# One gate for all tokens in expert 0's first steps, the routing maximum in PSUM, and a third head step before the last routing's products

## The chip, the cores and the metric

The kernel runs on one NeuronCore of one Trainium2 chip. The metric is device time in microseconds (us) of one launch, the median of the runs; lower is better. The engines are named as the profile names them: PE (TensorE's matmuls; PEld its weight loads), DVE (VectorE), ACT (ScalarE), POOL (GpSimd) and SP (SyncE, which issues most transfers). The granted clock in the profile's rows is a share of TensorE's full rate: 1.00 is 2.4 GHz, 0.50 is 1.2 GHz.

## The reference

Three layers follow one another.

1. A linear attention with a decay for each channel: 4 sequences of 768 tokens, 8 heads of width 48. Per token, `y = r · (state + (u*k) v^T)` and `state = w * state + k v^T`. The result is a matrix `x` of 3072 tokens by 384.
2. A mixture of 8 experts with one expert for each token. `logits = x @ w_gate` and `e_idx = argmax(logits)`. The token's output is `relu(x @ w1[e]) @ w2[e]`, multiplied by the softmax probability of the chosen expert and by `sigmoid(x @ w_output_gate)[e]`. The product of these two factors is what is called the gate value below.
3. A dense gated layer on all tokens: `(silu(x @ w_gate) * (x @ w_val)) @ w_out`, inner width 1536, from weights given as 64-bit floats.

All in 32-bit floats.

## The kernel before

**Attention.** The 3072 tokens are 24 tiles of 128 (`NTILE`), six for each sequence (`NCH`). One loop of 27 iterations runs all stages of the tiles in a skewed order, and inside it the order of the instructions of PE, DVE, ACT and POOL is the order of the program (`manual_schedule`). In iteration `i`, POOL makes products for tile `i+2` (`scaled_k`, L456 to L461), DVE reduces them to `cb` for tile `i+1` and ACT spreads them (`bonus`, L482 and L486), PE makes the scores and outputs (`scores`, `outputs`), and tile `i-2` is written out (`rows_out`, which runs `emit`). `emit` (L122) transposes the tile's result with 32 small matmuls into the PSUM tile `psx`; ACT copies the tokens (`xt`, L127, which SP then stores to `x_d`) and the partial logits (`lh`, L130), and DVE sums these to `lg` (L132): 8 routing logits and 8 logits of the output gate for each token.

**Routing.** When the six tiles of a sequence are done, the generator `route` is put on a list. Each call of `advance` runs one step of the first generator on that list, so the routing's small DVE instructions lie between those of the attention. A step marked TENSOR issues matmuls and runs only where `advance(TENSOR)` is called. `route` takes the row maximum (L144, `mx`), compares (L147, `key`), makes the one-hot `oh`, the counts `cum` (L167), a first group of products for the ranks (`psp`, L171 to L184), some arithmetic, and a second group of products (`psw`, L219) that gives the token lists `rows_f`. Most of its small tiles lie in one PSUM bank (`in_bank`). POOL's operands are all in SBUF.

**Gates.** `gate` (L230) makes the gate values of a group of tiles from `lg` and `mx`: 14 DVE instructions and two exponentials on ACT. For the sequences 0 and 1 it is put on the same list behind their routing. For the sequences 2 and 3 (12 tiles) the logits and the maximum lie at the end of a large SBUF tile (`lg_far`, `mx_far`, L567 and L568), and one gate over both runs in expert 0's first steps, three pieces in each step (`next(gates, None)` in `MoE.run`).

**Expert 0's head.** The first 256 tokens of expert 0 come from the first three sequences, so they are gathered and multiplied while the last sequence is still routed. `moe.head` is a generator of 8 steps, one for each 128 of the inner width 1024. Step `f` issues 9 matmuls into `pha` (L1208; two PSUM buffers in turn), a relu on ACT (L1227), a low part on DVE (L1228), and, from the third step on, the 9 matmuls of step `f-2` into `pya`. Behind the loop the order is by hand: seven pieces of the last routing, two head steps, the products for the ranks, five pieces, a head step, three pieces, a head step, the second products, two pieces (L671 to L680). Then the other tokens of expert 0 are gathered, `in_order` sorts the experts in steps that alternate with head steps, and the gathered tokens are transposed.

**Weights.** Operands of the experts are split in a high part (a cast on ACT, L1084) and a low part (a subtraction, L1085, here on POOL). For expert 0 this is done in the last iterations; `SPLITS` says which parts in which iteration.

**Experts and dense layer.** From there a scheduler orders the instructions by a simulated timeline: 8 experts with 416 to 360 tokens, beside them the conversion of the 64-bit weights, then the dense layer in blocks of 512 tokens.

Of the kernel before, what the change touches and what calls it, by code (L numbers as in the profile page):

```python
# [38 lines left out]
def moe_kernel(ctx, tc, cst, small, tok, tr, u, w1, w2, m_gate, m_val, m_out, out):  # L39
# [79 lines left out]
    def emit(yT, x_rows, lg, pool, ps_x):  # L119


        psx = ps_x.tile([P, 2, 8, 64], F32, name="psx", tag="x")  # L122
        for q, (j, k) in itertools.product(range(NP), ((0, 0), (1, 1), (0, 1), (1, 0))):
            pr, ts = slice(64 * j, 64 * j + 64), slice(64 * k, 64 * k + 64)
            nc.tensor.matmul(psx[ts, j, q, :], lhsT=yT[pr, q, ts], rhs=unit[pr, q, :], start=True, stop=True)
        xt = pool.tile([P, NP, 2, D], F32, name="xt")
        nc.scalar.copy(xt.rearrange("p q j d -> p j q d"), psx[:, :, 0:NP, 0:D])  # L127
        nc.sync.dma_start(out=x_rows, in_=xt.rearrange("p q j d -> p (q j d)"))
        lh = pool.tile([P, 2, NP, G], F32, name="lh")
        nc.scalar.copy(lh, psx[:, :, 0:NP, D:])  # L130
        yield
        nc.vector.reduce_sum(lg, lh.rearrange("p j q e -> p e (j q)"), axis=AX.X)  # L132
# [97 lines left out]
    def gate(sl, lg, mx, pool, sm):  # L230
# [3 lines left out]
        bc = lambda t: t.rearrange("p (c o) -> p c o", o=1).to_broadcast([P, n, E])  # L234
        ex = pool.tile([P, n, E], F32, name="ex")
# [67 lines left out]
    def scratch(pool, **kw):  # L303
        return lambda name, *dims: pool.tile([P, *dims], F32, name=name, **kw)


    with ExitStack() as actx:
# [95 lines left out]
        def tables():  # L403

            nc.gpsimd.memset(ones_b, 1.0)
            nc.gpsimd.memset(yd_all[:, used[0] :], 0.0)
# [158 lines left out]
        routing, gates, now = [], [], [0]  # L565
        far = slice(NTILE - 2 * NCH, NTILE)
        lg_far = yd_all[:, KD * YW - 2 * NCH * G :].rearrange("p (c g) -> p c g", g=G)  # L567
        mx_far = yd_all[:, KD * YW - 2 * NCH * (G + 1) : KD * YW - 2 * NCH * G]  # L568
        assert used[0] <= KD * YW - 2 * NCH * (G + 1)
# [22 lines left out]
        def rows_out(i):  # L592
            g = next(g for g in groups if g.start <= i < g.stop)
            n, late = g.stop - g.start, g.stop > NTILE - NCH
            if i == g.start:
                at = i - far.start
                if at < 0:
                    lgs[i] = apool.tile([P, n, G], F32, name="lg"), in_bank("mx", n)
                else:
                    lgs[i] = lg_far[:, at : at + n, :], mx_far[:, at : at + n]  # L600
            lg, mx = lgs[g.start]
            yield from emit(S.pop(i), x_d[i * P : (i + 1) * P, :], lg[:, i - g.start, :], apool, ps_x)
            if i + 1 == g.stop:
                routing.append((route(g, lg, mx, apool, in_bank, in_bank), 0, 0))
                if late:
                    gates.append((far, lg_far, mx_far))
                elif g.stop == NTILE - NCH:
                    routing.append((head_tokens(), 0, 0))
                else:
                    routing.append((gate(g, lg, mx, apool, in_bank), 0, 0))  # L610
# [10 lines left out]
        with tc.manual_schedule(engines=set(engines)):  # L621
# [50 lines left out]
            next(head)  # L672
            next(head)
# [11 lines left out]
            for _ in range(KF - 4):  # L685
                next(order, None)
                next(head)
            both = ps_x.tile([P, 2, 512], F32, name="pt01", tag="x")
# [91 lines left out]
    moe.run(sorted_positions, lambda pool: (x for g in gates for x in gate(*g, pool, scratch(pool))), ffn)  # L780
# [660 lines left out]
SPLITS = {21: ((0, 0),), 22: ((0, 1),), 23: ((1, 0), (1, 1)), 24: ((2, 0), (2, 1)), 25: ((3, 0),), 26: ((3, 1),)}  # L1441
# [113 lines left out]
```

## Time and profile before

| What | us |
|---|---|
| Median of 3 runs (801.03, 801.21, 805.11) | 801.21 |
| The profiled execution, its own time | 802.04 |
| The profiled execution, span from first to last instruction | 800.3 |
| PE busy in the span | 780.0 |
| DVE busy | 500.8 |
| ACT busy | 346.9 |
| POOL busy | 218.6 |

The busy times are shares of the whole span and mix stages with different limits: the attention up to about 122 us, the head of expert 0 to about 145, the experts to about 345, the dense layer to the end. The section with rows below is by stretch. In a timeline a line is: start, duration, engine, line of the kernel, operation, tiles with their shape, how many instructions were joined, and in brackets how long the engine had stood idle before it and what ended that.

### The profile page before, as it was taken

The numbers are of one execution on the slowest core, as the hardware profiler recorded it, in microseconds if no ns is written. First come the engines' busy times: TensorE is split into PE (matmuls) and PEld (weight loads), VectorE is DVE, ScalarE is ACT, GpSimd is POOL, SyncE is SP. The second block draws the span as 40 slices with busy tenths as digits, with TensorE's granted clock in tenths as the row PEclk, the third lists the DMA queues.
The fourth block names the chain that finished last, engine by engine and source line by source line (L and its number), as shares of the span: only waits on it lengthen the run. The fifth ranks groups of instructions, "written<-read, shape, count | busy, mean of one in ns | idle before, by whom it ended". The sixth has DMA issues, their size and how long they took to land.

```text
span 800.3 us, 15595 instructions
## 1 busy us (share of the span) xinstructions
PE 780.0 (97%) x5982; PEld 717.0 (90%) x5983; DVE 500.8 (63%) x1067; ACT 346.9 (43%) x789; POOL 218.6 (27%) x213
## 2 busy tenths in 40 slices
PE   8989988999999999999999999999999999999997
PEld 4888878999999999988888888888888888899997
DVE  7889976789999899788553335334433543344543
ACT  5878772656566666655332122212221222122322
POOL 6999975535232422120002000200100020001000
PEclk8999998999999999999999999999999999999999
DMA  8999972966778785564301000000000000000000
GB/s 322 309 340 304 332 245 95 316 201 203 262 230 256 234 248 175 152 180 141 107 15 40 1 0 14 40 1 0 36 18 1 8 40 1 1 8 40 1 20 25
DMA packets 61860, 99.28 MB, mean 124 GB/s; under 512 B 5461, under 2 KB 48105, under 8 KB 61776
## 3 DMA queue, kind: packets, MB, share of 16 engines
q1 hardware_dynamic: 58320, 88.34, 33.8%
q0 software_dynamic: 3456, 9.85, 3.7%
q8 instruction: 49, 0.80, 0.4%
q14 instruction: 35, 0.29, 0.1%
HBM read 81.64 MB, written 16.53 MB: 123 GB/s over the span
## 4 chain that ended last, share of the span: by engine, by line
issue 54%; PE 16%; DVE 6%; POOL 4%; DMA 3%; ACT 1%; POOLq 0%; SPq 0%; DVEq 0%; ACTq 0%
PE ph L1208 6%; PE py L1208 5%; POOL out_dram L1380 2%; DMA rw<-m 1%; DMA m<-ab 1%; PE pya L1208 1%; PE pha L1208 1%; DVE ab L1059 1%; PE pt L1177 1%; DVE w1l L1085 1%; POOL xg L1163 1%; DVE w2l L1085 1%; POOL x L1056 1%; DVE ab L1055 1%; PE ph L1204 1%
## 5 line engine op out<-in xcount | busy, mean ns | idle before, releaser
L1404 PE MATMUL pg<-x,wh 128*128 128x512 f32 (+1 forms) x504 | 146.5, 358 | 0.0
L1409 DVE TENSOR_TENSOR hv<-pg,hv 128x512 f32<-128x512 f32 (+1 forms) x84 | 51.5, 614 | 142.0 <-ACT hv L1408 141.9
L1404 PE MATMUL pv<-x,wh 128*128 128x512 f32 (+1 forms) x504 | 137.7, 358 | 0.0
L1380 POOL DMA_INDIRECT out_dram<-ot,tokd x24 | 24.9, 1036 | 407.3 <-DVE ot L1379 403.7
L1408 ACT ACTIVATE hv<-pg 128x512 f32<-128x512 f32 (+1 forms) x84 | 45.0, 536 | 158.8 <-PE pg L1404 158.5
L974 ACT CAST hh<-hv 128x512 fp32r<-128x512 f32 (+1 forms) x84 | 47.0, 560 | 136.7 <-DVE hv L1410 136.7
L1404 PEld LDWEIGHTS pv<-x,wh 128*128 128x128 f32 x504 | 89.9, 188 | 13.9
L1404 PEld LDWEIGHTS pg<-x,wh 128*128 128x128 f32 x504 | 90.2, 188 | 11.3
L1371 PE MATMUL po<-wh,hl 128*128 128x384 f32 x288 | 97.1, 338 | 0.0
L1371 PE MATMUL po<-wh,hh 128*128 128x384 f32 x288 | 96.8, 336 | 0.0
L1371 PE MATMUL po<-wl,hh 128*128 128x384 f32 x288 | 96.8, 336 | 0.0
L1404 PE MATMUL pg<-x,wl 128*128 128x512 f32 (+1 forms) x252 | 90.3, 358 | 0.0
L1404 PE MATMUL pv<-x,wl 128*128 128x512 f32 (+1 forms) x252 | 90.3, 358 | 0.0
L1208 PE MATMUL ph<-x,w1h 128*128 128x416 f32 (+6 forms) x336 | 87.5, 341 | 0.0
L1208 PE MATMUL py<-h,w2h 128*128 128x416 f32 (+6 forms) x336 | 82.3, 341 | 0.0
L975 DVE TENSOR_TENSOR hl<-hv,hh 128x512 fp32r<-128x512 f32 (+1 forms) x84 | 51.7, 615 | 43.6 <-ACT hh L974 43.3
L1410 DVE TENSOR_TENSOR hv<-pv,hv 128x512 f32<-128x512 f32 (+1 forms) x84 | 51.6, 615 | 38.9 <-PE pv L1404 38.3
L486 ACT ACTIVATE dsb<-cs,cb 128x128 f32<-128x128 f32 x192 | 58.8, 389 | 19.5 <-DVE cb L482 19.4
L1208 PEld LDWEIGHTS ph<-x,w1h 128*128 128x128 f32 x336 | 61.5, 188 | 0.2
L1208 PEld LDWEIGHTS py<-h,w2h 128*128 128x128 f32 x336 | 60.7, 188 | 0.5 <-DVE h L1228 0.3
L1056 POOL TENSOR_TENSOR low<-low,exw 128x384 f32<-128x384 f32 x30 | 33.0, 1101 | 98.8 <-DVE exw L1052 78.7
L1208 PE MATMUL ph<-x,w1l 128*128 128x416 f32 (+6 forms) x168 | 58.4, 347 | 0.5 <-DVE h L1228 0.5
(254 smaller groups left out, 1509.8 us busy)
## 6 DMA issues: line engine op xcount, KB each, us to landing
r<-in_w_dram SPq DMA_DIRECT2D x64, 384.0 KB, 4.2
yd_all<-in_tr_dram SPq DMA_DIRECT2D x24, 512.0 KB, 5.2
yd_all<-in_tok_dram SPq DMA_DIRECT2D x24, 384.0 KB, 5.7
rw<-m SPq DMA_DIRECT2D x36, 192.0 KB, 2.7
yd_all<-in_tok_dram SPq DMA_DIRECT2D x24, 256.0 KB, 5.8
m<-ab SPq DMA_DIRECT2D x30, 192.0 KB, 4.4
x_d<-xt SPq DMA_DIRECT2D x24, 192.0 KB, 4.3
cva<-in_w_gate_dram SPq DMA_DIRECT2D x10, 384.0 KB, 4.5
```

The costliest lines, as they stand in the source:

```text
L486: nc.scalar.mul(dsb[:, h, :], ident, cb[:, h : h + 1])
L974: first = nc.scalar.copy(hi, src)
L975: second = nc.vector.tensor_tensor(out=lo, in0=src, in1=hi.bitcast(F32), op=ALU.subtract)
L1056: nc.gpsimd.tensor_tensor(out=low, in0=low, in1=ex.bitcast(F32), op=ALU.mult)
L1085: (engine or nc.vector).tensor_tensor(out=lo, in0=r, in1=hi.bitcast(F32), op=ALU.subtract)
L1208: nc.tensor.matmul(dst[:, 0:n], lhsT=a, rhs=b, start=start and t == 0, stop=stop and t == 2)
L1371: mm = nc.tensor.matmul(po[t], lhsT=a[:, t * P : (t + 1) * P], rhs=bb, start=(f == 0 and j == 0), stop=(f == KF2 - 1 and j == 2))
L1380: st = nc.gpsimd.indirect_dma_start(out=out[:, :], out_offset=bass.IndirectOffsetOnAxis(ap=tokd[:, i : i + 1].bitcast(U32), axis=0), in_=o ...
L1404: nc.tensor.matmul(dst, lhsT=a[:, fs], rhs=bb[:, q, :], start=(q == 0 and j == 0), stop=(q == KD - 1 and j == 2))
L1408: nc.scalar.activation(hv, pg, AF.Sigmoid)
L1409: nc.vector.tensor_tensor(out=hv, in0=pg, in1=hv, op=ALU.mult)
L1410: nc.vector.tensor_tensor(out=hv, in0=pv, in1=hv, op=ALU.mult)
```

## The change

- `emit`: ACT copies `lh` before `xt`; the store of `xt` is issued behind both.
- `rows_out`: for all four sequences the logits lie at the end of the large SBUF tile (`lg_all`, 24 tiles) and the maximum lies in the PSUM bank. No gate is put on the list any more.
- `gate` is called once, over all 24 tiles, in expert 0's first steps. It is given no maximum and takes its own, into SBUF.
- The memset of the large tile's end on POOL leaves out the part where the logits lie.
- Behind the loop three head steps, not two, stand before the products for the ranks, and one fewer behind the second products; `in_order` is finished after the third of these.
- `SPLITS`: the casts and subtractions of expert 0's weight group 2 move from iteration 24 to 25, and the first half of group 3 from 25 to 26.

```diff
@@ emit
+        lh = pool.tile([P, 2, NP, G], F32, name="lh")
+        nc.scalar.copy(lh, psx[:, :, 0:NP, D:])
         xt = pool.tile([P, NP, 2, D], F32, name="xt")
         nc.scalar.copy(xt.rearrange("p q j d -> p j q d"), psx[:, :, 0:NP, 0:D])
         nc.sync.dma_start(out=x_rows, in_=xt.rearrange("p q j d -> p (q j d)"))
-        lh = pool.tile([P, 2, NP, G], F32, name="lh")
-        nc.scalar.copy(lh, psx[:, :, 0:NP, D:])
@@ gate
+        if mx is None:
+            mx = pool.tile([P, n], F32, name="mx")
+            nc.vector.reduce_max(mx, gl, axis=AX.X)
@@ tables
-            nc.gpsimd.memset(yd_all[:, used[0] :], 0.0)
+            nc.gpsimd.memset(yd_all[:, used[0] : KD * YW - NTILE * G], 0.0)
@@ rows_out
-                at = i - far.start
-                if at < 0:
-                    lgs[i] = apool.tile([P, n, G], F32, name="lg"), in_bank("mx", n)
-                else:
-                    lgs[i] = lg_far[:, at : at + n, :], mx_far[:, at : at + n]
+                lgs[i] = lg_all[:, g, :], in_bank("mx", g.stop - g.start)
...
-                if late:
-                    gates.append((far, lg_far, mx_far))
-                elif g.stop == NTILE - NCH:
+                if g.stop == NTILE - NCH:
                     routing.append((head_tokens(), 0, 0))
-                else:
-                    routing.append((gate(g, lg, mx, apool, in_bank), 0, 0))
@@ behind the loop
             urgent(7)
-            next(head)
-            next(head)
+            for _ in range(3):
+                next(head)
             urgent(1, TENSOR)
...
-            for _ in range(KF - 4):
+            for _ in range(KF - 5):
                 next(order, None)
                 next(head)
+            for _ in order:
+                pass
@@ the call of the experts
-    moe.run(sorted_positions, lambda pool: (x for g in gates for x in gate(*g, pool, scratch(pool))), ffn)
+    moe.run(sorted_positions, lambda pool: gate(slice(0, NTILE), lg_all, None, pool, scratch(pool)), ffn)
@@ SPLITS
-SPLITS = {21: ((0, 0),), 22: ((0, 1),), 23: ((1, 0), (1, 1)), 24: ((2, 0), (2, 1)), 25: ((3, 0),), 26: ((3, 1),)}
+SPLITS = {21: ((0, 0),), 22: ((0, 1),), 23: ((1, 0), (1, 1)), 25: ((2, 0), (2, 1)), 26: ((3, 0), (3, 1))}
```

## Rows read from the trace of the kernel before

**Rows 1.** Windows: length, PE, PEld, DVE, ACT, POOL, clock, DMA, GB/s; last PE alone.

```profile
80.00:100.00 20.00, 18.61 (x416) 16.40 (x414) 19.01 (x60) 15.70 (x52) 19.44 (x19) 1.00 0.93 331
...
126.00:132.20 6.20, 6.17 (x36) 6.11 (x36) 3.94 (x13) 0.38 (x1) 2.00 (x2) 0.50 0.26 91
...
147.50:160.00 12.50, 12.50 (x97) 12.28 (x96) 12.42 (x39) 10.14 (x28) 4.67 (x5) 1.00 0.92 312
160.00:170.00 10.00, 10.00 (x63) 9.69 (x62) 7.86 (x19) 5.90 (x14) 4.47 (x4) 1.00 0.81 267
170.00:320.00 150.00, 150.00 (x864) 147.84 (x863) 140.56 (x268) 92.34 (x178) 50.82 (x43) 1.00 0.73 224
...
14.00:16.00 2.00, 2.00 (x26) 0.50 1.03 400
```

**Rows 2.** Timeline of PE, 9 to 16 us and 119 to 146 us.

```profile
13.20 2.08 PE L499 MATMUL pss<-rdT,kdT 64*128 64x128 f32 x16 [2.26 <-DVE rdT L470]
...
120.10 0.69 PE L125 MATMUL psx<-unit,yT 64*64 64x64 f32 x32 [0.83 <-ACT lh L130]
...
126.00 0.20 PE L171 MATMUL bank<-oh_all,mask_b 128*128 128x48 bf16 x1 [2.90 <-DVE cum L167]
...
135.76 0.28 PE L1208 MATMUL pha<-x,w1l 128*128 128x256 f32 x1
...
137.87 0.28 PE L1208 MATMUL pha<-x,w1l 128*128 128x256 f32 x1
```

**Rows 3.** Timeline of DVE, 119 to 127 us.

```profile
122.09 0.38 DVE L132 TENSOR_REDUCE yd_all<-lh 128x16 f32<-128x128 f32 x1 [1.63 <-ACT lh L130]
...
122.74 1.80 DVE L147 TENSOR_TENSOR bank<-yd_all 128x48 f32<-128x48 f32 x1
...
125.79 0.16 DVE L167 TENSOR_TENSOR cum<-cum,bank 128x8 bf16<-128x8 bf16 x1
125.87 0.75 DVE L1228 SCALAR_TENSOR_TENSOR h<-pha,h 128x256 fp32r<-128x256 f32 x2
```

**Rows 4.** Instructions of line 147: ns min/median/max, first and last start, form.

```profile
L147 DVE TENSOR_TENSOR bank<-lg,bank x2: 203/204/204, 47.9 to 73.9; 128x48 f32<-128x48 f32 x2
L147 DVE TENSOR_TENSOR bank<-yd_all x2: 802/1300/1798, 99.7 to 122.7; 128x48 f32<-128x48 f32 x2
```

**Rows 5.** Timeline of POOL, 100 to 146 us.

```profile
107.30 1.82 POOL L1085 TENSOR_TENSOR w1l<-r,w1h 128x768 fp32r<-128x768 f32 x1 [1.45 <-ACT w1h L1084]
...
122.66 1.80 POOL L1085 TENSOR_TENSOR w2l<-r,w2h 128x768 fp32r<-128x768 f32 x1
```

**Rows 6.** Timeline of DVE, 84 to 92 us: first gate instruction, then `cb`.

```profile
88.07 0.19 DVE L236 TENSOR_TENSOR ex<-lg,bank 128x48 f32<-128x48 f32 x1
...
91.06 0.51 DVE L482 TENSOR_REDUCE cb<-ck 128x8 f32<-128x384 f32 x1
```

**Rows 7.** Timeline of ACT, 86 to 103 us and 119 to 125 us.

```profile
91.60 2.45 ACT L486 ACTIVATE dsb<-cs,cb 128x128 f32<-128x128 f32 x8 [1.60 <-DVE cb L482]
...
121.40 0.49 ACT L127 COPY xt<-psx 128x384 f32<-128x384 f32 x1
...
121.92 0.86 ACT L1084 CAST w1h<-r 128x768 fp32r<-128x768 f32 x1
...
123.39 0.69 ACT L1227 ACTIVATE h<-pha 128x256 fp32r<-128x256 f32 x2
```

**Rows 8.** Instructions of the lines 406, 248 and 211, whole span.

```profile
L406 POOL MEMSET yd_all<- x1: 1132/1132/1132, 26.1 to 26.1; 128x1244 f32 x1
...
L248 DVE RECIPROCAL room<-room x1: 744/744/744, 149.5 to 149.5; 128x96 f32<-128x96 f32 x1
...
L211 DVE TENSOR_TENSOR bank<-cs,bank x4: 353/359/363, 57.7 to 130.5; 128x192 f32<-128x192 f32 x4
```

**Rows 9.** Transfers of 118 to 165 us (issues, us to landing), and line 1056.

```profile
xg<-x_d,rows_m POOLq DMA_INDIRECT x2, 2.8
...
L1056 POOL TENSOR_TENSOR low<-low,exw x30: 1010/1118/1588, 173.6 to 321.9; 128x384 f32<-128x384 f32 x30
```

More of the change, by code (lines that the diff above doesn't have):

```diff
@@ L564, in moe_kernel @@
         groups = [slice(b * NCH, (b + 1) * NCH) for b in range(B)]
[L565 to L569, printed above, removed]
+        routing, now = [], [0]
+        lg_all = yd_all[:, KD * YW - NTILE * G :].rearrange("p (c g) -> p c g", g=G)
+        assert used[0] <= KD * YW - NTILE * G
         def advance(tensor=0):
@@ L593, in rows_out @@
             g = next(g for g in groups if g.start <= i < g.stop)
-            n, late = g.stop - g.start, g.stop > NTILE - NCH
             if i == g.start:
-                at = i - far.start
-                if at < 0:
-                    lgs[i] = apool.tile([P, n, G], F32, name="lg"), in_bank("mx", n)
-                else:
-                    lgs[i] = lg_far[:, at : at + n, :], mx_far[:, at : at + n]
+                lgs[i] = lg_all[:, g, :], in_bank("mx", g.stop - g.start)
             lg, mx = lgs[g.start]
```

## The prediction

> **What bounds the kernel now.** I read first which engine is busy in which stretch, then the order of instructions where TensorE stands still, then for each neighbour what it waits for. In the attention stage GpSimd is the full engine: from 80 to 100 us it is busy 19.44 of 20 us and VectorE 19.01 of 20 [rows 1]. From 145 us on TensorE is: it is busy 10.00 of 10 us from 160 to 170 and 150.00 of 150 from 170 to 320 [rows 1]. A microsecond that TensorE reaches that stage earlier is therefore a microsecond of the total, unless something in the stage itself becomes late. The change works at the seam, 100 to 160 us. There the timeline of TensorE shows one hole: after expert 0's first two head steps it stands still for 2.90 us, 123.10 to 126.00, until VectorE has written `cum` [rows 2]. Behind the hole the granted clock is 0.50, the 1.2 GHz level, for the 6.2 us from 126.0 to 132.2 with 6.17 us of work in them [rows 1]: that work would take half as long at 2.4 GHz, so 3.1 us are lost there beside the 2.90.
>
> Why is `cum` late? VectorE's list for the last routing has one odd entry: the `is_equal` of L147 takes 1.80 us, 122.74 to 124.54 [rows 3]. Its four executions are the evidence: twice 0.20 us with the maximum in PSUM, 0.80 and 1.80 us with the maximum in SBUF, same shape [rows 4]. The 1.80 us end 0.08 us after a GpSimd subtraction that ran from 122.66 to 124.46 [rows 5].
>
> **Term 1, the end of the attention: -1.2 us (0 to -1.8).** Taking the two gates out of the routing removes 28 VectorE and 4 ScalarE instructions. While GpSimd runs without a pause that is worth nothing, since it sets the pace. It counts at the end. Seven gate instructions of group 1, from 88.07 on, stand ahead of the `cb` reduction at 91.06 [rows 6], and ScalarE waits 1.60 us for that reduction [rows 7]. Without them ScalarE is up to 1.60 us earlier from there on, and the routing of group 2 also saves 0.60 us on its L147 (0.80 to 0.20). What can be kept of both: GpSimd, done with the attention's products, stands 1.45 us before its first weight subtraction at 107.30, waiting for ScalarE [rows 5]. It cannot begin that earlier than 105.85, so 1.45 us is the most. The smaller memset on GpSimd (1244 to 860 columns) takes away 0.35 of its 1.13 us [rows 8], perhaps kept. Lower end: nothing, if VectorE stays late for another reason. I take 1.2, nearer the GpSimd pause, because both savings lie on the path to it.
>
> **Term 2, the hole: 2.90 to 2.1 us, so -0.8 us (-1.6 to +0.4).** Step by step, on the clock of the old run:
> - The last attention tile's products end at 120.79 [rows 2]. ScalarE read them only at 121.40, because two weight casts of group 2 stood before [rows 7]. With these casts moved one iteration on, and `lh` copied ahead of `xt`, `lh` is there at 121.13, not 122.06, so VectorE's reduction starts at 121.15, not 122.09 [rows 3].
> - L147 takes 0.20 instead of 1.80. So `cum`, which ended at 125.95 [rows 3], ends at 125.95 - 0.94 - 1.60 = 123.4. VectorE is then no longer what ends the hole.
> - What is late next: the third head step, now ahead of the routing's products, writes a PSUM buffer of which there are two, so it waits until the first step's result is read by ScalarE (relu) and by VectorE. The relu has four weight casts before it (groups 2 and 3), not one. Casts and relu follow each other every 0.735 us (121.92 to 123.39 in two) [rows 7]. After `xt`, at 121.36, four of them put the first relu at 124.30, where it was at 123.39. It takes 0.38, VectorE's low part another 0.4 [rows 3], and TensorE goes on at 125.2. The hole is 125.2 - 123.1 = 2.1 us.
> - The routing's products then stand behind a whole head step of 18 matmuls (2.11 us at full clock, 135.76 to 137.87 [rows 2], twice that at half). They come later than at 126.00, but TensorE has work before them and one head step fewer after them. The gather of the other tokens is covered by three head steps, 6.3 us, not four, and lands 2.8 us after its issue [rows 9]: no price.
>
> The ends: -1.6 if the relu comes in as early as before, +0.4 if VectorE does its first two low parts only after later work. The x_d store, now behind two copies, is late by one `lh` copy (0.28 us); its readers gather many microseconds later.
>
> **Term 3, the clock after the hole: -1.4 us if it falls again, -3.1 if it does not.** Two holes of the trace bear on it: 2.90 us here, and 2.26 us at 13.20 [rows 2], behind which the clock is 0.50 as well [rows 1]. The 0.83 us at 120.10 cost nothing [rows 2]. My 2.1 us lie next to the shorter of the two that fell, so I expect a fall, with a chance of 7 in 10. What it costs then lies between nothing and the 3.1 us of before. I take half the way, 1.7 us lost, since the timed runs have a median of 801.21 and the profiled execution took 802.04: the 0.83 between them, if it is a shorter slow stretch (an estimate), says that 3.1 is at the long end.
>
> **Term 4, the wide gate: +0.9 us (0 to +1.7).** The gate of 12 tiles in expert 0's steps becomes one of 24, with a maximum of its own. From 96 to 192 elements: the reciprocal goes from 0.74 to about 1.3 us [rows 8], an elementwise step grows by 0.11 (0.20 at 48 elements [rows 4], 0.36 at 192 [rows 8]). Reciprocal +0.57, three products +0.11 each, two sums +0.11 each, the add +0.08, the new maximum 0.35, seven narrow steps +0.02 each: +1.7 us on VectorE. That engine is full there, 12.42 of 12.50 us from 147.5 to 160, and has 2.1 us free in the next ten [rows 1]. So the backlog is paid back by 170, and the question is how much TensorE, now without a pause, waits in between. Between nothing and all 1.7: the middle. On ScalarE the two exponentials widen by under 0.1 us each, beside other work. `in_order`'s last part, moved behind the third step, only has later readers.
>
> The rule that speaks against this part is in the Trainium skill, "SBUF — State Buffer", section "Who interferes with whom": a VectorE instruction with two inputs in SBUF waits out a GpSimd instruction that reads SBUF, while a reduction or one with a PSUM input does not. For L147 the rows above say the same, 0.20 against 0.80 and 1.80 us. It bears equally on the wide gate, whose difference and two products have both inputs in SBUF; what follows if it bites is the third rival.
>
> **The sum.** The profiled execution took 802.04 us, a span of 800.3 and 1.7 around it. 802.04 - 1.2 - 0.8 - 1.4 + 0.9 = 799.5 us, that is 1.7 below the median of 801.21. About 0.5% (4 us) is what a measurement of this kernel can tell from no change, so I forecast a small gain that counts as "same".
>
> **Rivals.**
> - *The clock stays up.* Term 3 is then -3.1: 802.04 - 1.2 - 0.8 - 3.1 + 0.9 = 797.8 us. For it: the hole is shorter than both that fell, and term 1 does not lengthen it. Against: only by 0.16 us than the shorter one. Chance 0.20.
> - *The attention's end gains nothing*, because GpSimd keeps its own pace: its products alone fill the stage, and the reader of ScalarE's early casts is GpSimd. Term 1 is 0: 800.7 us. Against: the 1.45 us in which it stands idle before 107.30. Chance 0.21.
> - *The wide gate is blocked, and the kernel is slower.* Place: the difference and the two products of L236, L253 and L258, each with two SBUF inputs, in 147 to 158 us. If a GpSimd product that reads SBUF (1.1 us, L1056 [rows 9]) runs beside each, VectorE loses 3.3 us besides the 1.7, and having no free time there it hands 5.0 to TensorE: 802.04 - 1.2 - 0.8 - 1.4 + 5.0 = 803.6 us. It makes the kernel slower than 801.21 once terms 1 to 3 (3.4 less the 0.83) are outdone, from a loss of 2.6 us on. Against: the first of these GpSimd products starts at 173.6 [rows 9], and the scheduler would have to bring them forward. Chance 0.10.
>
> My forecast keeps 0.49. A gain above 0.5% (under 797.2) needs the raised clock with most of term 1 and little of term 4: 0.13. A loss above 0.5% (over 805.2) needs the blocked gate and a long slow stretch: 0.04. The rest, 0.83, lies within. The range reaches from a little below the second case, 796.9, to the middle of the bounds of term 4 and the nearer part of the blocked case, 802.4. The forecast's own range, by terms 2 to 4, is 798.2 to 801.0.
>
> **What would show it.** Right: L147 at 0.20 us in the last routing, `lh` ahead of `xt`, the last `cum` some 2.5 us earlier against the end of the last attention products; a TensorE hole of about 2 us before the third head step, released by VectorE's low part and not by `cum`; GpSimd's pause before its first weight subtraction shorter by a microsecond. VectorE still full past 160, with waits of TensorE between 147 and 160 that sum to about 1 us. Wrong: a hole ended by something else or longer than 2.9 us; a clock of 1.00 all through 120 to 135 (first rival); the first weight subtraction still at 107 (second); single gate instructions of a microsecond (third). The prediction as a whole fails if the scheduler, which orders the expert stage anew, makes TensorE wait after 160.

## The result and the profile after

| | us |
|---|---|
| Kernel before, median | 801.12 |
| Changed kernel, median (806.46 to 810.34) | 808.18 |
| Ratio, 95% interval | 1.0080 [1.0054, 1.0107] |
| Profiled execution after, its own time and its span | 807.29, 805.5 |

The forecast was 799.5 us with a range of 796.9 to 802.4. The kernel became 0.8% slower, and the time lies outside the range. In the timeline of TensorE the forecast order of events holds up to 140.76 us, and then the engine stands still (start, duration, engine, line, operation; in brackets the idle time before it and what ended it):

```profile
117.53 0.69 PE L125 MATMUL psx<-unit,yT 64*64 64x64 f32 x32 [0.83 <-ACT xt L129]
...
122.80 0.36 PE L1202 MATMUL pha<-x,w1l 128*128 128x256 f32 x1 [2.27 <-DVE h L1222]
...
148.07 0.64 PE L1198 MATMUL ph<-x,w1h 128*128 128x320 f32 x1 [7.31 <-ACT yd_all L1246]
...
353.90 0.39 PE L1398 MATMUL pg<-x,wl 128*128 128x512 f32 x1
```

The last attention products come at 117.53 (120.10 in [rows 2]), the hole is 2.27 us (2.90) and ends with the low part of step 1, as predicted. The head's last product ends at 148.07 - 7.31 = 140.76, some 4.4 us ahead of the old run. Then TensorE waits 7.31 us for ScalarE to copy `pya` out of PSUM. The last line is the first product of the dense layer. The same two places in the trace of the kernel before:

```profile
145.36 0.41 PE L1204 MATMUL ph<-x,w1h 128*128 128x320 f32 x1 [0.17 <-ACT yd_all L1252]
...
348.90 0.39 PE L1404 MATMUL pg<-x,wl 128*128 128x512 f32 x1
```

ScalarE after, in the same stretch:

```profile
140.13 0.24 ACT L968 CAST x<-bank 128x96 fp32r<-128x96 f32 x1 [1.47 <-PE pya L1202]
147.38 0.92 ACT L1246 COPY yd_all<-pya 128x256 f32<-128x256 f32 x3 [7.01 <-remote]
```

ScalarE stands idle too, 7.01 us, until something called "remote". That word only means that no event of this trace fits the end of the wait. The trace of before has no such entry. The copy waits for two counts, one of TensorE and one of GpSimd. The trace's records of TensorE's counter show its last three steps at 147.30, 147.35 and 147.40, although the three products of `pya` that make them ended at 140.05, 140.41 and 140.76. The work was done; the news of it came up to 7.25 us late, in a bundle. SyncE's issues of expert 1's weight loads were slow in the same time:

```profile
137.27 0.40 SPq L1067 DMA_DIRECT2D r<-in_w_dram  x1
137.93 0.38 SPq L1071 DMA_DIRECT2D r<-in_w_dram  x1
139.34 0.71 SPq L1067 DMA_DIRECT2D r<-in_w_dram  x1
140.14 0.37 SPq L1071 DMA_DIRECT2D r<-in_w_dram  x1
142.24 0.69 SPq L1067 DMA_DIRECT2D r<-in_w_dram  x1
143.02 0.64 SPq L1071 DMA_DIRECT2D r<-in_w_dram  x1
145.08 0.70 SPq L1067 DMA_DIRECT2D r<-in_w_dram  x1
147.22 0.00 SPq L1071 DMA_DIRECT2D r<-in_w_dram  x1
```

In the old trace these eight come 0.61 to 0.65 us apart (139.58 to 143.95). Here they take 10 us, and each stop between two instructions of SyncE, also between plain register instructions, is about 0.70 us. SyncE goes on freely from 147.22, TensorE's counts arrive from 147.30.

The windows that answer to [rows 1] (length, busy time of PE, PEld, DVE, ACT, POOL, granted clock, DMA share, GB/s):

```profile
80.00:100.00 20.00, 19.36 (x440) 17.02 (x436) 18.40 (x54) 16.13 (x52) 19.24 (x19) 1.00 0.94 321
126.00:132.20 6.20, 6.20 (x58) 6.16 (x55) 4.40 (x17) 0.77 (x2) 1.07 (x2) 0.87 0.00 0
147.50:160.00 12.50, 11.77 (x77) 11.23 (x78) 8.71 (x26) 7.18 (x23) 1.81 (x2) 0.84 0.34 118
160.00:170.00 10.00, 10.00 (x68) 9.55 (x67) 9.56 (x25) 7.96 (x19) 5.45 (x6) 1.00 0.86 262
170.00:320.00 150.00, 150.00 (x864) 147.76 (x863) 139.74 (x269) 91.94 (x180) 51.09 (x44) 1.00 0.76 234
```

Behind the idle the clock is partly at the lower level (0.84 from 147.5 to 160, where it was 1.00): an estimate of 0.16 x 12.5 = 2.0 us lost there, beside the idle itself. Past 160 TensorE is full again at 1.00.

### The profile page after: what moved, and what is told of

Same layout as the page of the kernel before. It is cut to its first block, busy times and chain, and to the rows that moved or that the text cites. A ratio compares the mean times of both kernels' runs of the same rounds, so it can differ in the third digit from the quotient of the medians.

```text
span 805.5 us, 15589 instructions
## 1 busy us (share of the span) xinstructions
PE 779.2 (97%) x5982; PEld 715.8 (89%) x5983; DVE 497.2 (62%) x1040; ACT 347.7 (43%) x785; POOL 219.7 (27%) x213
## 4 chain that ended last, share of the span: by engine, by line
issue 54%; PE 25%; DVE 8%; POOL 4%; DMA 4%; ACT 2%; another core or an unknown queue 1%; SPq 1%; POOLq 0%; ACTq 0%; DVEq 0%
PE ph L1202 6%; PE py L1202 5%; PE pss L502 3%; PE psy L550 2%; PE psy L558 2%; POOL out_dram L1374 2%; PE psx L125 2%; PE pskv L524 1%; DMA rw<-m 1%; DMA m<-ab 1%; PE pya L1202 1%; PE pha L1202 1%; DMA m<-x 1%; DMA yd_all<-in_tok_dram 1%; DVE w2l L1079 1%
```

## The experiments

The experiments fell on four chips, here A to D. The ratio, with its interval, is always to runs of the kernel before on the same chip, over all runs of both, and so differs a little from the quotient of the two medians; the old kernel's medians there were 801.59 (A), 802.26 (B), 801.85 and 801.94 (C), 801.23 (D). "Late" says whether the trace shows counts of TensorE that come microseconds after their products.

| run | chip | median us | ratio [95%] | late |
|---|---|---|---|---|
| e1_again | A | 799.29 | 0.9973 [0.9959, 0.9986] | no |
| e1_gates_only | A | 797.72 | 0.9954 [0.9936, 0.9973] | no |
| e1_head_only | A | 801.08 | 0.9996 [0.9977, 1.0014] | no |
| e1_order_late | A | 802.17 | 1.0006 [0.9992, 1.0020] | no |
| e2_again | B | 810.79 | 1.0093 [1.0061, 1.0125] | yes |
| e2_g_lh | B | 800.80 | 0.9982 [0.9965, 0.9998] | yes |
| e2_g_splits | B | 801.67 | 0.9994 [0.9976, 1.0012] | yes |
| e2_g_steps | B | 808.24 | 1.0063 [1.0037, 1.0089] | yes |
| e3_again | C | 809.27 | 1.0086 [1.0061, 1.0111] | yes |
| e3_order_late | C | 807.96 | 1.0070 [1.0046, 1.0093] | yes |
| e3_loads_late | C | 816.42 | 1.0171 [1.0140, 1.0201] | yes |
| e3_gathers_late | C | 805.83 | 1.0035 [1.0017, 1.0054] | yes |
| e4_before | C | 804.06 (one) | | yes |
| e4_again | C | 813.40 (one) | | yes |
| e4_gates_only | C | 801.57 | 0.9992 [0.9980, 1.0005] | yes |
| e4_mx_only | C | 801.21 | 1.0005 [0.9984, 1.0026] | yes |
| e5_order_early | D | 798.61 | 0.9973 [0.9961, 0.9984] | no |
| e5_g_early | D | 797.68 | 0.9943 [0.9924, 0.9962] | no |

### The changed kernel again, and its two halves

**e1_again**, no edit.

> The changed kernel once more, nothing edited. The profile after shows TensorE idle for 7.31 us between expert 0's last head product and the first product of its next step, with ScalarE's copy of pya let go at 147.38 although the products ended by 140.77. Theory A (the place: the new order lets something block there in every execution): 806 to 810 us again, and an idle of 5 to 9 us in the same place. Theory B (it belongs to that one profiled execution): the idle at that place is under 1 us in this profile, and the time lost, if it is lost, shows elsewhere or in a different stretch of each profile.

It took 799.29 us, 0.2 us from the forecast, on chip A. That nearness is in part luck: in this execution the clock stayed at 1.00 behind the hole, as in the first rival (797.8 us), and the other terms fell short of theirs (the table further down). Its TensorE timeline:

```profile
119.16 0.69 PE L125 MATMUL psx<-unit,yT 64*64 64x64 f32 x32 [0.83 <-ACT xt L129]
...
124.43 0.36 PE L1202 MATMUL pha<-x,w1l 128*128 128x256 f32 x1 [2.27 <-DVE h L1222]
...
141.09 0.42 PE L1198 MATMUL ph<-x,w1h 128*128 128x320 f32 x1 [0.17 <-ACT yd_all L1246]
...
345.83 0.40 PE L1398 MATMUL pg<-x,wl 128*128 128x512 f32 x1
```

The same hole to the hundredth, and where 7.31 us were lost 0.17 are. ScalarE's copy there follows its product at once, and SyncE's issues come 0.62 us apart:

```profile
140.31 1.02 ACT L1246 COPY yd_all<-pya 128x256 f32<-128x256 f32 x3 [1.34 <-PE pya L1202]
```

```profile
138.09 0.38 SPq L1071 DMA_DIRECT2D r<-in_w_dram  x1
138.72 0.37 SPq L1067 DMA_DIRECT2D r<-in_w_dram  x1
139.34 0.37 SPq L1071 DMA_DIRECT2D r<-in_w_dram  x1
139.96 0.37 SPq L1067 DMA_DIRECT2D r<-in_w_dram  x1
```

So the idle does not follow from the order of the instructions alone. Theory A as put there is refuted on chip A.

**e1_gates_only**, the change without its head part:

```diff
-        lh ... ahead of xt        +        lh ... behind xt
-            for _ in range(3):    +            next(head); next(head)
-            for _ in range(KF - 5):  ... for _ in order: pass
+            for _ in range(KF - 4):
-SPLITS = {..., 25: ((2, 0), (2, 1)), 26: ((3, 0), (3, 1))}
+SPLITS = {..., 24: ((2, 0), (2, 1)), 25: ((3, 0),), 26: ((3, 1),)}
```

> The changed kernel with lh behind xt, the old order of weight casts and two head steps before the last routing's products, so that only the one wide gate and the maximum in PSUM are left of the change. Theory A1 (the stall comes from the head that ends 4.4 us earlier, through the third head step and the finished order of experts): no stall, TensorE at expert 0's transposes 1 to 3 us earlier than before, 799 to 801 us. Theory A2 (the stall or loss comes from the gate part: DVE's work and the order that the scheduler makes behind it): 805 us or more, with the idle between head and steps.

**e1_head_only**, the kernel before with just those lines of the head part.

> The kernel before with lh ahead of xt, the new order of weight casts and three head steps before the last routing's products; the gates and the maximum stay as before. Theory A1 (the stall comes from the head part): 805 us or more, with 5 us or more of idle of TensorE after the last pya product. Theory A2 (from the gate part): no such idle, 799 to 802 us.

The gates part alone gave 797.72 us, a lower median than all of the change, though the two intervals overlap; the head part alone 801.08, no gain that the interval tells. Neither shows the idle, so on this chip theories A1 and A2 are not told apart. TensorE with the gates part alone:

```profile
117.86 0.69 PE L125 MATMUL psx<-unit,yT 64*64 64x64 f32 x32 [0.83 <-ACT lh L130]
...
122.19 0.18 PE L171 MATMUL bank<-oh_all,mask_b 128*128 128x48 bf16 x1 [1.32 <-DVE cum L167]
...
138.90 0.42 PE L1196 MATMUL ph<-x,w1h 128*128 128x320 f32 x1 [0.17 <-ACT yd_all L1244]
```

With L147 at 0.21 us the old order's hole is 1.32 us, ended by `cum`. The head part turns that into 2.27, because it puts four weight casts ahead of the first relu and a step that needs this relu ahead of the products that don't. From the last `psx` line to the first product of expert 0's other steps it is 138.90 - 117.86 = 21.04 us against 141.09 - 119.16 = 21.93 with the head part, both at a clock of 1.00: there the head part costs 0.9 us. Its new order of casts also takes GpSimd out of the way of L147: in e1_head_only the last L147 still has both operands in SBUF and takes 0.22 us, since GpSimd stands idle beside it, and the hole is 2.21 us all the same.

**e1_order_late**, `in_order` moved behind the whole head:

```diff
             for _ in range(KF - 5):
-                next(order, None)
                 next(head)
-            for _ in order:
-                pass
...
             for _ in head:
                 pass
+            for _ in order:
+                pass
```

> The changed kernel with the sort of the experts (in_order) moved behind the whole head, so that the loads of expert 1's weights and the gathers of its tokens, which need its result, are issued some 4 us later. Theory A3 (the stall is made by these loads and gathers running while the head's last products hand over their results): the idle after the last pya product shrinks to under 2 us, ScalarE's copies follow the products within 0.5 us, and the time is 799 to 803 us. Theory A4 (it has nothing to do with when these transfers start): 806 us or more with the idle in the same place.

With nothing late on this chip it showed only its price: 802.17 us, TensorE busy 10.24 of 12.5 us from 147.5 to 160 since expert 1's weights and tokens come late.

### On a second chip: which edit brings the idle

**e2_again**, no edit.

> The changed kernel a third time, nothing edited, to see whether the idle of 7.31 us after the last pya product and the late hand-overs of TensorE's results come back. Theory B (they belong to a single session, not to the order of the instructions): 797 to 801 us, no idle over 1 us after pya, and a hole before the third head step of 2.27 us ended by the low part of step 1, behind which the granted clock may stay at 1.00 or fall. Theory A (the order has a race for a resource that is lost in some sessions): 806 to 810 us with late hand-overs again.

810.79 us, with the idle (7.29 us). Theory B missed in its number: the idle is not a single event of one execution.

**e2_g_lh, e2_g_splits, e2_g_steps**: the gates part with one edit of the head part each (`lh` first; the new SPLITS; three head steps with `in_order` finished behind the third of the later ones).

> Only the wide gate and the maximum in PSUM, and lh copied ahead of xt; old order of casts, two head steps before the routing's products. The profile with the first two edits alone has a hole of 1.32 us ended by cum, and xt's copy of 0.37 us in front of the last lh. If cum is what ends the hole there, it shrinks to 0.9 to 1.1 us and the time falls by 0 to 0.5 us against the 797.72 of those two edits; if the order of the two copies does not matter, the hole stays at 1.3.

> Only the wide gate, the maximum in PSUM and the new order of weight casts (group 2 and the first half of group 3 one iteration later). Theory C (the order of casts makes the hole of 2.27 us, since four casts of 0.74 us stand ahead of the first relu, but with two head steps the routing's products don't need that relu): the hole before the routing's products is ended by cum, 0.6 to 1.4 us, a second one follows before the third head step (the relu is some 1.5 us later), together 1.8 to 2.5 us, and the time is 0.5 to 1.5 us over the 797.72 without this edit. Rival: the order of casts relieves the attention's last iterations, the last attention products end earlier by 0.5 us or more, and the time is 797 or less.

> Only the wide gate, the maximum in PSUM and the three head steps before the routing's products, with the old order of casts (two of them ahead of the first relu, not four). Theory D (the third step itself costs nothing if the relu is early): the hole is ended by step 1's low part at about the time that cum ended it, 1.2 to 1.5 us, the routing's products follow 2.1 us later without a hole of their own, and the time is within 0.6 us of the 797.72 without this edit. Rival (the products that come later delay the tokens' gather or the experts' order): a new idle before expert 0's transposes or in its first steps, 0.7 us or more, and 798.5 or more.

Two of the holes came as expected: 0.95 us with `lh` first; 0.81 and 1.08 with the new casts (theory C). With three steps and the old casts it was 1.73, ended by GpSimd's `w2l`, where theory D expected 1.2 to 1.5 and VectorE. The times were set by something else. With three steps alone the idle is there:

```profile
124.00 0.36 PE L1202 MATMUL pha<-x,w1l 128*128 128x256 f32 x1 [1.73 <-POOL w2l L1079]
...
147.76 0.63 PE L1198 MATMUL ph<-x,w1h 128*128 128x320 f32 x1 [7.30 <-ACT yd_all L1246]
```

With either of the other two edits it is not (0.38 and 0.46 us at that place), though their traces also show late counts and SyncE's 0.70 us stops. So on a chip of this kind the edit that brings the 7.3 us is the third head step ahead of the routing's products, with which `in_order` is finished by hand. Not every execution has it: nine of the ten of e2_g_steps took 806.35 to 811.78 us, and one took 801.62.

### On a third chip: what the idle hangs on

**e3_again** (no edit), **e3_order_late** (as e1_order_late), and two that move one kind of transfer each:

```diff
# e3_loads_late: the first expert's number reaches SyncE behind ScalarE's first copy of pya (new tiles' lines left out)
+            nc.vector.scalar_tensor_tensor(out=late, in0=yd_all[:, 0:E], scalar=0.0, in1=ids, op0=ALU.mult, op1=ALU.add)
+            nc.vector.tensor_copy(ids2, late)
-    nc.sync.value_load(env["ids"][...
+    nc.sync.value_load(env["ids2"][...
# e3_gathers_late: the same for the token lists that GpSimd's gathers read
+        nc.vector.scalar_tensor_tensor(out=late, in0=yd_all[:, 0 : E * NJ], scalar=0.0, in1=rows_k, op0=ALU.mult, op1=ALU.add)
-        nc.vector.tensor_copy(rows, rows_k)
+        nc.vector.tensor_copy(rows, late)
```

> The changed kernel once more as the mark for this chip. On one chip it took 799.3 us without any late hand-over, on another 810.8 with an idle of 7.29 us after pya. If the state belongs to the chip, this one shows one of the two clearly: 797 to 801 with no idle over 1 us, or 806 to 812 with an idle of 7.2 to 7.4 us. If it is drawn anew for each load of the program, times between runs of this label mix both.

> The sort of the experts moved behind the head, so that the loads of expert 1's weights and the gathers of its tokens start some 4 us later. Where the changed kernel shows the idle of 7.3 us: theory E (the state is set off by the two kinds of transfers starting together while TensorE still hands over the head's results) expects pya's copies within 1 us of the products and 801 to 804 us; theory F (an idle of fixed length wherever the head ends) expects 809 or more. Where the changed kernel is undisturbed: about 802 as measured before, because expert 1's weights come late.

> The changed kernel with the number of the first expert handed to SyncE only after ScalarE's first copy of pya (two small VectorE instructions more, one of them reading yd), so that expert 1's eight weight loads start some 4 us later; the gathers stay. Where the changed kernel shows the idle: theory E1 (SyncE's weight loads set it off) expects the copies within 1 us of the products and 800 to 804 us; theory E2 (the gathers do) expects the idle unchanged and 808 or more. Where it is undisturbed: 799 to 802 us, TensorE waiting up to 2.5 us for expert 1's weights.

> The changed kernel with the token lists of the experts written only after ScalarE's first copy of pya, so that the gathers of expert 1 and 2 start some 5 us later; the weight loads stay. Where the changed kernel shows the idle: theory E1 (the weight loads set it off) expects the idle unchanged and 807 or more; theory E2 (the gathers, or both together) expects it gone and 800 to 803. Where it is undisturbed: 798 to 801 us.

The mark showed the idle, 7.30 us. In each of the other three `pya` is copied at once (TensorE idle 0.16 or 0.17 us there), so with these transfers moved the idle at that place is gone. That it needs both kinds is not shown: e3_loads_late also delayed the gathers, whose first is issued 2.0 us ahead of the head's end there and 4.9 us ahead in the mark. The onset points to the gathers. In all thirteen late traces SyncE's first instruction or pause of some 0.6 to 0.7 us comes 2.1 to 3.5 us after the first of the eight gathers that follow `ids`. The loads are no such mark: in e3_gathers_late seven of them go out 0.61 to 0.65 us apart from 137.96 on and the slow steps begin near 145, behind the first gather at 142.46; in e3_loads_late a register instruction of SyncE takes 0.63 us at 143.27, ahead of the first load at 143.91. But the times missed what was expected (807.96, 816.42, 805.83), since the late counts only go elsewhere. The ten executions of e3_gathers_late lie in two groups, 802.96 to 804.88 and 806.78 to 807.87, and in e3_loads_late the dense layer also takes 4.2 us longer than in the old trace (455.6 against 451.4); neither was followed up. ScalarE with late gathers, and with the late sort:

```profile
140.84 1.02 ACT L1250 COPY yd_all<-pya 128x256 f32<-128x256 f32 x3 [1.34 <-PE pya L1206]
...
153.96 0.49 ACT L1222 COPY hs<-ph 128x160 f32<-128x160 f32 x2 [3.27 <-remote]
```

```profile
141.97 1.02 ACT L1245 COPY yd_all<-pya 128x256 f32<-128x256 f32 x3 [1.34 <-PE pya L1201]
...
155.97 0.48 ACT L967 CAST x<-pt 128x384 fp32r<-128x384 f32 x1 [5.11 <-remote]
```

Delay is no cure: the late stretch follows the transfers, and now hits expert 0's later steps.

### The kernel before on such a chip

**e4_before** and **e4_again** are the two kernels unedited; **e4_gates_only** repeats e1_gates_only; **e4_mx_only** is the kernel before with `gate` taking its own maximum where it is given none (the lines `if mx is None` of the change) and this:

```diff
-                    lgs[i] = lg_far[:, at : at + n, :], mx_far[:, at : at + n]
+                    lgs[i] = lg_far[:, at : at + n, :], in_bank("mx", n)
-                    gates.append((far, lg_far, mx_far))
+                    gates.append((far, lg_far, None))
```

> The kernel before, for its trace on this chip; 800 to 804 us. On two of three chips every changed order so far shows TensorE's results handed over up to 7.3 us late while expert 1's weight loads run, and SyncE's instructions in steps of 0.70 us; the medians of the kernel before on the three chips are 801.6, 802.3 and 801.9. Theory G1 (the chip does the same to the kernel before, at places where TensorE has other work): on a chip of that kind its trace shows steps of 0.70 us of SyncE in 139 to 150 us and late hand-overs that cost under 1 us. Theory G2 (the old order keeps clear of it): SyncE's loads 0.63 us apart as in the trace of before, and no late hand-over, though the next run of this call shows the idle.

> The changed kernel as the mark of this chip: 797 to 801 us without, or 806 to 812 with the idle of 7.3 us after pya.

> Only the wide gate and the maximum in PSUM, on another chip than the first time (797.72 us and 0.9954 of before there, without late hand-overs). If this chip is of the disturbed kind: its near relatives with lh ahead (0.9982) and with the new order of casts (0.9994) say 0.995 to 1.000 of before, with late hand-overs that fall into the head while TensorE still has work; if the last pya hand-over is hit instead, 1.005 or more. If not disturbed: 0.993 to 0.997 again.

> The kernel before with the maximum of the last two groups in PSUM too (the far gate takes its own); the first two gates stay in the attention, all else as before. Theory H1 (the maximum in PSUM is what shortens the hole): L147 at 0.20 us, the hole before the routing's products 1.0 to 1.5 us where it was 2.90, and where not disturbed 0.3 to 0.5% faster than before, nearly all of what the two edits give together. Theory H2 (most of that comes from the gates taken out of the attention): hole 1.0 to 1.5 us too, but the attention's end stays where it was and the time is within 0.25% of before.

Theory G1 holds in kind: on chip C the kernel before has late counts too. Its TensorE, ScalarE, SyncE and line 147:

```profile
125.02 0.18 PE L171 MATMUL bank<-oh_all,mask_b 128*128 128x48 bf16 x1 [1.40 <-DVE cum L167]
...
142.05 0.41 PE L1204 MATMUL ph<-x,w1h 128*128 128x320 f32 x1 [0.38 <-issue]
...
147.13 0.42 PE L1204 MATMUL ph<-x,w1h 128*128 128x320 f32 x1 [1.89 <-DVE hs L1225]
...
350.87 0.39 PE L1404 MATMUL pg<-x,wl 128*128 128x512 f32 x1
```

```profile
139.57 0.38 ACT L1227 ACTIVATE h<-pha 128x256 fp32r<-128x256 f32 x1 [3.67 <-issue]
...
146.43 0.29 ACT L1224 COPY hs<-ph 128x160 f32<-128x160 f32 x1 [3.04 <-PE ph L1205]
```

```profile
137.36 0.27 SPq L1073 DMA_DIRECT2D r<-in_w_dram  x1
138.80 0.01 SPq L1077 DMA_DIRECT2D r<-in_w_dram  x1
139.51 0.00 SPq L1073 DMA_DIRECT2D r<-in_w_dram  x1
```

```profile
123.27 0.28 DVE L147 TENSOR_TENSOR bank<-yd_all 128x48 f32<-128x48 f32 x1
```

A relu comes some 2 us after its product, but inside the head, where TensorE has two more steps of work; a second late stretch costs 1.89 us. From the head's end to the dense layer this execution needs 350.87 - 142.05 = 208.8 us, 5.3 more than the undisturbed old one (348.90 - 145.36 = 203.5). Besides the 1.89 us there is the clock behind that wait, 0.68 from 147 to 152 us and 0.78 from 152 to 160. It is only 2.0 us longer than that in span (802.3 against 800.3), because this time L147 met only the last 0.21 us of a GpSimd subtraction (it took 0.28 us, hole 1.40, clock 1.00 behind it). G1's "under 1 us" was too low for this execution. Yet the kernel before has nearly the same median on all four chips, 801.23 to 802.26, so the 5.3 us of one execution is not what such a chip costs it as a rule; what makes up for it is not shown.

The maximum in PSUM alone gave 1.0005 and the whole gates part 0.9992 on this chip; the intervals overlap, so H1 and H2 are not told apart.

### Does the distance decide?

In all five traces with the long idle (after, e2_again, e2_g_steps, e3_again, e4_again) the head's last product ends 3.5 us behind the first issue of expert 1's loads (140.76 - 137.27 above), and ScalarE's copy starts 10.07 to 10.11 us behind it (147.38 - 137.27). In the late traces without it the distance is 5.6 to 6.4 us, or a kind of transfer had been moved by hand (in e3_gathers_late the distance is 3.5 us too, but the gathers stand behind the head). Counted from the first gather it is 4.9 us in the five and 7.0 to 7.8 in the others, so the two marks move together. Two kernels move the distance. **e5_order_early** is the changed kernel, **e5_g_early** the gates part alone, both with:

```diff
                 next(order, None)
+                next(order, None)
                 next(head)
```

> The changed kernel with two pieces of in_order ahead of each of the next head steps, not one, so that the first expert's number is there one head step (2.1 us) earlier, as in the kernel before. In every trace with the idle of 7.3 us the last pya product ends 3.48 us after the issue of expert 1's first weight load, and its hand-over comes 10.0 us after that issue; in the traces of the same chips without that idle the distance is 5.6 to 6.4 us and the hand-over 0.3 us late. Theory J (that distance decides): distance 5.6 us, copies of pya within 0.7 us of the products, no idle of 7 us; on a disturbed chip 800 to 804 us, on the other 797 to 800. Theory K (the third head step ahead of the routing's products does it in another way, through the order on TensorE or ScalarE): on a disturbed chip the idle of 7.3 us stays, 807 to 811.

> Only the wide gate and the maximum in PSUM, and two pieces of in_order ahead of each head step, so that expert 1's loads start another head step earlier: distance from the first load to the end of the last pya product about 7.7 us. Theory J: on a disturbed chip this puts the last hand-over into the second stretch of late hand-overs (between 6.5 and 10 us after the first load, as the hand-over of ph at 7.1 us that came 3.35 us late in the trace of the kernel before), so an idle of 1.5 to 3 us there and 800 to 804 us, no better than the 0.9992 of before without this edit; on the undisturbed chip within 0.3 us of the 797.72. Rival: the earlier the loads, the more of the late hand-overs falls into the head where TensorE has work, and the kernel gains 1 us or more (0.998 of before or less on a disturbed chip).

Chip D turned out to be one without late counts, so theories J and K are not told apart. The distances became 4.8 us (5.6 were expected) and 6.9 (7.7 were expected). The times are 798.61 us, as the changed kernel on chip A, and 797.68, the best ratio of all (0.9943), though its interval overlaps that of the gates part alone.

## Why the prediction was wrong

Along the path of TensorE the two executions of the changed kernel compare with the old one as follows, each difference from the rows above and [rows 2]:

| part of the path | forecast | e1_again | after |
|---|---|---|---|
| attention's last products (120.10) | -1.2 | -0.94 | -2.57 |
| hole (2.90) | -0.8 | -0.63 | -0.63 |
| from the hole to the head's last product (clock) | -1.4, or -3.1 | -2.70 | -1.23 |
| idle behind that product (0.17) | 0 | 0.00 | +7.14 |
| expert steps up to the dense layer (wide gate) | +0.9 | +1.20 | +2.29 |
| dense layer | 0 | +0.2 | +0.2 |
| sum (span) | -2.5 | -2.9 | +5.2 |

**Term 1** right in sign and, on chip A, in size, and GpSimd's pause before its first weight subtraction (1.45 us in [rows 5]) went as predicted. After, and in e1_again:

```profile
104.98 1.83 POOL L1079 TENSOR_TENSOR w1l<-r,w1h 128x768 fp32r<-128x768 f32 x1
106.80 1.83 POOL L1079 TENSOR_TENSOR w1l<-r,w1h 128x768 fp32r<-128x768 f32 x1 [0.29 <-ACT w1h L1078]
```

It is a noisy place: in the 16 traces with the gates taken out the last `psx` row starts at 117.5 to 123.1, 119.4 in the mean, in the four with the gates in the attention at 120.1 to 122.2, mean 121.0. The 2.57 of one execution is not the effect; the mean, 1.6, is near the bound.

**Term 2** right, with its mechanism: relu behind four casts, hole 2.27 for 2.1. L147 takes 0.20 us in all four executions of the trace after:

```profile
L147 DVE TENSOR_TENSOR bank<-yd_all,bank x4: 204/205/213, 47.2 to 119.3; 128x48 f32<-128x48 f32 x4
```

That agrees with the Trainium skill, "SBUF — State Buffer", section "Who interferes with whom": a tensor-tensor instruction of VectorE with at most one input in SBUF does not contend with GpSimd. In this trace a GpSimd product ran beside the first three; at the fourth (119.29) GpSimd stood idle, and the better proof is e4_mx_only, where a weight subtraction (123.60 to 125.41) ran beside the last L147 and it took 0.21. But the 1.80 us in [rows 4] was one draw: without the maximum in PSUM the last L147 took 0.28 in e4_before and 0.22 in e1_head_only. The gain counted from 2.90 us was larger than in those.

**Term 3**: eleven traces have a hole of 2.21 to 2.27 us there; the clock fell behind it in seven and stayed at 1.00 in four, close to the 7 in 10 that I gave. A fall costs 1.4 to 1.5 us: from the hole's end to the head's last product it is 17.96 us after and 16.5 in e1_again, for the 1.7 taken. So the old trace's slow stretch had cost 2.7 us, not 3.1: that is what e1_again gained by staying at 1.00.

**Term 4**: +1.20 for +0.9 in e1_again, within its bounds, and the third rival did not come: the wide reciprocal took 1.35 us (1.3 was estimated), the difference L239 0.35, so no gate step was held up. That all of it is the wide gate is not shown: between 141 and 160 us TensorE has one wait on VectorE of more than 0.15 us,

```profile
147.45 0.42 PE L1198 MATMUL ph<-x,w1h 128*128 128x320 f32 x1 [0.43 <-DVE hs L1219]
```

and e1_head_only, with the narrow gate, is 0.4 us longer there than the old trace as well. Of the +2.29 in the recorded execution most is the lower clock behind the idle (2.0 us by the estimate above).

**What failed** is the path behind the head: the sum has no term for the hand-over from the head's last product to expert 0's other steps, 0.17 us before, and it took 7.31. Term 2 moved a head step ahead of the routing's products, saw "one head step fewer after them", and priced only the gather of the other tokens. But the same step also leaves only one head step, not two, between the write of `ids`, the experts' order, and the head's end. VectorE writes `ids` before, then after, and SyncE's first load before:

```profile
138.01 0.17 DVE L296 CAST ids<-ids_f 128x8 int32<-128x8 f32 x1
135.69 0.17 DVE L299 CAST ids<-ids_f 128x8 int32<-128x8 f32 x1
139.58 0.40 SPq L1073 DMA_DIRECT2D r<-in_w_dram  x1
```

SyncE's eight weight loads of expert 1 follow `ids` by 1.6 us in both, and GpSimd's gathers by 0.2 us. So the loads began 3.5 us ahead of the head's end, not 5.6, and the gathers 4.9, not 7.0 (e1_head_only, with the head part alone, has 3.5 from the loads too, and e1_gates_only 5.6), and I gave that no price. The sentence on `in_order`'s last part is not the fault: that part, the counts, is read by later sorting steps of VectorE. On chips B and C, and in the recorded run, TensorE's results are then handed over only about when SyncE is through with these loads. e2_g_steps shows that the third head step brings the idle of 7.30 us, and e1_again that without the chip's late counts the same kernel lands at 799.29. None of the four cases had it: the rival on the slower side had the wrong place and mechanism, and all of them took the expert stage to begin when the head's last product ends.

**What stays open.** Whether the distance decides (3.5 us from the first load, 4.9 from the first gather) or the third step does it otherwise; whether the gathers alone set off the late counts or the loads are needed too; and what makes counts late on chips B and C and not on A and D. Only chip C was used at two times, so for the other three the chip and the time of the runs are not told apart. The DMA throughput is the same (347 GB/s from 139 to 147.5 after, 355 in e1_again). The traces with late counts also lack records: of VectorE's 1001 counter steps in the trace after 969 are recorded, in e1_again all of them. A path shared by counts and records would fit that; it is not shown. The Trainium skill has a rule of that kind ("NOTIFIC — the notification-queue block", "7.1 Overflow: three behaviours, one of which stalls the engine"): when its ring is full, the block that writes the profiler's records can, in one of three settings, hold up whatever produces them, and by it the late counts would belong to the recording. The same table has the loss of new records as another setting, so the lost records by themselves do not speak for it. No run here can show it, since each has its span and clock from that recording.

## What to carry to other kernels

A step that is moved ahead is missing behind: ask what now lies closer together there, follow each result written in that stretch into every queue, and look at what the transfers that it starts will meet, above all at a point where the next engine has no other work. Take the price of a stall from more than one execution (a collision of 1.80 us was 0.28 in another), and measure a gain of half a per cent on more than one chip: the same kernel was 0.27% faster on one and 0.9% slower on two others, while the gates part alone was slower on neither of its two (0.9954 and 0.9992).

## What the runs showed of the hardware

- On two of four chips, beginning 2.1 to 3.5 us after the first of the eight gathers that follow `ids`, TensorE's counts reach the other engines up to 7.25 us after the product, and SyncE advances in stops of about 0.70 us, some ten of them in 9 us. ScalarE's and VectorE's own steps there are prompt: after, VectorE starts its part of `x` 0.03 us after ScalarE's cast ends (140.40 against 140.37).
- In the five traces that have it (one is the recorded run, whose chip is not known) the idle is 7.28 to 7.31 us, equal to within 0.03 us.
- A PSUM operand in L147 gave 0.20 to 0.21 us in every trace that has it, beside whatever GpSimd did; with both operands in SBUF the same instruction took 0.22 to 1.80. The length is what was left of the GpSimd instruction that ran when it started: in five executions (0.28, 0.60, 0.80, 1.30 and 1.80 us) it ended 0.07 to 0.08 us after that one, and the 0.22 us is the one with GpSimd idle.
